# The order of A sums, raw K's turn and the merge's turns on VectorE, in a recurrence followed by a mixture of experts

## The chip, the cores and the metric

The kernel runs on one core of a Trainium2 chip. The metric is the device time of one execution in microseconds. Before the change it is 1082.37 us, the median of 3 runs (1082.31 to 1082.71).

## The reference

The first block is a recurrence over 768 tokens, for 4 batches of 8 heads with head dimension 40. Each head carries a 40 x 40 state:

```python
for t in range(S):
    kt, vt, rt = (k[:, :, t], v[:, :, t], r[:, :, t])
    wt, at, bt = (w[:, :, t], a[:, :, t], b[:, :, t])
    y[:, :, t] = np.einsum('bhd,bhde->bhe', rt, state)
    Sa = np.einsum('bhde,bhe->bhd', state, at)
    state_decay = state * wt[:, :, None, :] - np.einsum('bhd,bhe->bhde', Sa, bt)
    state = state_decay + np.einsum('bhd,bhe->bhde', vt, kt)
```

Its output, 3072 tokens of 320 numbers, goes through a mixture of 4 experts with 1024 hidden columns. The weights p are the given probabilities, divided by their sum for each token:

```python
for e in range(E):
    h = np.maximum(x @ w1[e], 0.0)
    out += p[:, e:e + 1] * (h @ w2[e])
```

Everything is float32.

## The kernel before, in words

**Units and chunks.** The recurrence is cut into chunks of 64 tokens. A unit is one chunk of two of the four batches, so there are 24 units, numbered 0 to 23, and two units make a chunk. All 8 heads of a unit are worked on at once. Units 8 and later (`BY_CHANNEL`) turn their raw inputs K and B on VectorE; earlier ones go another way.

**What a unit does.** Four generators make the instructions of a unit, a stage at a time:
- `within`: the work that needs no state. G is the running product of the decays w (a turn of raw W, a scan), gp its reciprocal (L582). RT, VT and AT are turned from raw data by `turn_raw` (L324). NT is turned from raw B and multiplied by gp (L640), KT from raw K and multiplied by gp (L645). TensorE forms the scores pc (from RT and VT), pfe (NT, AT), pe (KT, AT) and pev.
- `substitute`: solves a unit triangular system in blocks of 32. VectorE forms M (L730 to L746); GpSimd then runs 16 rounds of one product (L760) and two additions (L777) on Z, some 22 us.
- `merge`: VectorE turns Z to Qc (L793) and Qc to QTc (L794); GpSimd copies QTc into QT (L800); TensorE computes pY from QTc, then pQ from Qc.
- `step`: the work with the state. TensorE computes prn, psat, pxr and pdy; VectorE forms RH (L844), Y (L913, L919) and the new state (L924, L925). Y goes by 8 transfers on SyncE's queue into xT, the input of the mixture.

**The mixture.** It runs by chunks, one chunk behind, in pieces put between the stages above. Hidden columns come in two halves: TensorE forms ph, ScalarE writes hs with the rectifier (L978). The down product uses seven products of half blocks in place of eight. `down_1` forms p431, three products in one PSUM tile; its third term reads the sum a1. `down_2` forms p75 and p26, which read the sums a7, a5, a2 and a6. VectorE forms these five A sums from hs (`add_h`, L1104, 128x512 each, one buffer for each of the five, so a sum of one expert can be written only when the product of the expert before has read it). It also adds each product, times the gate, into osb: four operations behind p431 (L993; for a chunk's first expert two of them are L991), four behind p75 and p26 (L993). PSUM tiles of the mixture share three slots.

**Order.** Each engine runs its instructions in the order in which they stand in its queue. A scheduler lays that order out from the program order and its priorities. On VectorE it is bound further by stated edges: `tc.add_manual_dep(..., BEHIND)` puts one instruction behind another on the engine without a wait. The list `ahead_of_merge` has such edges for the units from 8 on. In it, names such as `sum_a{n}`, `Kr{u}.0` (the first turn of raw K), `K{u}` and `N{u}` (the products with gp), `Qc{u}`, `QTc{u}` and `out{n}` (the additions into osb) stand for single instructions. Before the change it has, among others, these:

```python
    ahead_of_merge = [(f"{x}{u}", f"Qc{u - 1}") for u in range(BY_CHANNEL, NU) for x in "KN"]
    ahead_of_merge += [
        (f"{x}{u}", f"sum_a{10 * (u - 1) - 50 + n}") for u in range(BY_CHANNEL, NU) for x in "KN" for n in range(5)
    ]
```

So the products N and K of unit u go ahead of five sums, and ahead of the merge of unit u - 1. These five are the second set of sums in a loop body; the first set is bound by another edge, behind gp of a later unit. The main loop (`for u in range(1, NU)`) emits, for u of 5 or more: the stages of unit u's `step`, `gap(1)` (two pieces of the mixture), the first stage of the merge of unit u + 1, and so on.

Of the kernel before, what the change touches and what calls it, by code (L numbers as in the profile page):

```python
# [33 lines left out]
def kernel(  # L34
# [48 lines left out]
    NU = NC * B // 2  # L83
# [38 lines left out]
    def of_mixture(name):  # L122
# [6 lines left out]
        out=ident[:], in_=ident[:], pattern=[[1, P]], compare_op=ALU.is_equal, fill=0.0,  # L129
# [5 lines left out]
    for t, n, op in ((upf, L, ALU.is_gt), (diagf, Q, ALU.is_equal)):  # L135
        nc.vector.memset(t, 1.0)
        for q in range(P // n):
            o = slice(q * n, (q + 1) * n)
            nc.gpsimd.affine_select(
                out=t[o], in_=t[o], pattern=[[1, n]], compare_op=op, fill=0.0, base=0, channel_multiplier=-1,  # L140
# [71 lines left out]
    BY_CHANNEL = 8  # L212
# [101 lines left out]
    def go(moves, eng=None):  # L314
        for move in moves:
            move(eng or nc.sync)
# [471 lines left out]
    def merge(q):  # L788


        Qc = sb.tile([P, H, Q], FP32, name="Qc", tag="q", bufs=2)
        QTc = sb.tile([P, H, Q], FP32, name="QTc", tag="q", bufs=2)
        keep(noted(nc.vector.transpose(out=dealt(Qc[:]), in_=q.Z), "Qc", q.u))  # L793
        ins = nc.vector.transpose(  # L794
            out=QTc[:].rearrange("p h r -> p (h r)"), in_=Qc[:].rearrange("p h c -> p (h c)"),
        )
        keep(noted(ins, "QTc", q.u))
        q.QT = QTs()
        for i in range(P // Q):
            ins = nc.gpsimd.tensor_copy(out=q.QT[quarter(i), :, quarter(i % 2)], in_=QTc[quarter(i)])  # L800
            tc.keep_in_program_order(ins)
        yield

        def two_heads(name, lhsT, rhs, to):
            p = (of_mixture if q.u == 0 and name == "pY" else big)(name)
            for n in range(NJ):
                for r in range(2):
                    matmul(
                        out=p[half(r), n * 2 * Q:(n + 1) * 2 * Q], lhsT=lhsT[half(r), 2 * n:2 * n + 2, :],
                        rhs=rhs[half(r), 2 * n:2 * n + 2, :], start=True, stop=True,  # L810
                    )
            for r in range(2):
                for y in range(2):
                    src = p[quarter(2 * r + y), 0:H * Q].rearrange("p (n two t) -> p n two t", two=2, t=Q)[:, :, y, :]
                    with sooner(name == "pY"):
                        ins = nc.scalar.copy(out=of_slot(to[quarter(2 * r)], y), in_=src)
                    noted(ins, name + "c", q.u, 2 * r + y)

        Y = Ys()
        two_heads("pY", q.below, QTc, Y)  # L820
        yield

        two_heads("pQ", Qc, Y, q.QT[:, :, quarter(1)])
        yield
# [348 lines left out]
    def begin_later(n):  # L1173
        for move in later[:n]:
            tc.keep_in_program_order(move(nc.sync))
        del later[:n]

    def mix(n):

        for piece in todo[:n]:  # L1180
            ready = stores[:]
            del stores[:]
            piece()
            for begin_store in ready:
                begin_store()
            begin_later(6 if here[0] % 4 == 0 and n > 1 else 3 if n > 1 else 6)
        del todo[:n]
# [5 lines left out]
    def run(gen, n=99):  # L1193
        if gen is None:
            return
        for _ in range(n):
            if next(gen, gen) is gen:
                break
# [3 lines left out]
    def begin_step(u):  # L1202
        q = units[u]
        if q.bp == 0:
            chunks_x[q.c] = sb.tile([P, 3, 2 * P], FP32, name="xT", tag="xT", bufs=2)
        q.xT = chunks_x[q.c][:, :, q.bp * P:(q.bp + 1) * P]
        return step(q, q.xT)
# [40 lines left out]
    m, s = merge(units[0]), begin_step(0)  # L1248
# [37 lines left out]
    m, s = merge(units[1]), begin_step(1)  # L1286
# [24 lines left out]
    for u in range(1, NU):  # L1311
        in_order[0] = True
        q = units[u]
        m = s_next = w = w_next = iter(())
        if u + 1 < NU:
            m, s_next = merge(units[u + 1]), begin_step(u + 1)
            w_next = ws[u + 1]
        if u + 2 < NU:
            w = ws[u + 2]

        def gap(n, pieces=None):
            here[0] = at = 4 * u + n
            run(sum_ops, sums_at.get(at, 0))
            mix((1 if at in sparse else 2) if pieces is None else pieces)

        early = u < EARLY
        if early:
            begin_later(len(later))
        ahead = u + 3 < NU and u >= EARLY
        if ahead and u < EARLY + 3:  # L1330
            go(load_raw(begin(u + 3), "W"))
        if early:
            lead()
        if u == 1:
            run(s, 1)
            run(w_next)
        else:
            run(w_next, 99 if early else 1)
            if u == EARLY:
                lead()  # L1340
            run(s, 1)
        gap(0)


        if early:
            run(s, 1)
        run(w, 1)
        if not early:
            run(w_next)
            run(s, 1)  # L1350
            if BY_CHANNEL <= u + 2 < NU:
                load_tokens(units[u + 2])
            run(s)

        if early:
            run(w, 1)
            gap(1, 2 if u + 1 == EARLY else None)
            run(s)
        if u == 1:
            mixture_of_unit(q)  # L1360
        elif q.bp:
            mixture_of_chunk(units[u - 1:u + 1], chunks_x[q.c])
        if not early:
            begin_later(len(later))
            run(w, 1)
            lead()
            todo[:2] = todo[1::-1]
            gap(1)
            run(m, 1)

        if u + 3 < NU:
            if u == 1:
                go_now(load_raw(begin(4), "WVRA"))
            else:
                go(load_raw(units[u + 3] if ahead else begin(u + 3), "A" if ahead else "WA"))
            load(units[u + 3], "V" if u + 3 >= BY_CHANNEL else "WBKV")
            if u > 1:
                later.extend(load_raw(units[u + 3], "VR"))
        run(w, 2)
        if BY_CHANNEL <= u + 2 < NU:  # L1380
            scale_tokens(units[u + 2])

        soon = u in (2, 3, 4)
        if soon:
            run(w, 1)
        if early:
            run(m, 1)
        else:
            run(m, 1)
            run(s_next, 1)  # L1390
            lead()
            run(m, 1)
            if u + 3 < NU:
                ws.append(within(units[u + 3]))
                run(ws[u + 3], 1)
        if soon:
            substitute(units[u + 2], nc.gpsimd)
        gap(2)

        if u == 1:  # L1400
            run(s_next, 1)
            run(m, 1)
        if not soon:
            run(w, 1)
        if not soon and u + 2 < NU:
            with sooner(not early):
                substitute(units[u + 2], nc.gpsimd)
        if not early:
            lead()
            run(s_next, 1)  # L1410
        if early:
            run(w, 1)
        if early:
            ws.append(within(units[u + 3]))
            run(ws[u + 3], 1)
            if u > 1:
                run(m, 1)
                run(s_next, 1)
            run(m)
            if u == 3:  # L1420
                begin_later(len(later))
            gap(3, 1)
            run(s_next, 1)
        else:
            if BY_CHANNEL <= u + 3 < NU:
                if u + 3 == BY_CHANNEL:
                    pad_raw()
                later.extend(load_raw(units[u + 3], "BK"))
            begin_later(len(later))
            gap(3)  # L1430
        if u >= EARLY + 2 and u + 4 < NU:
            later.extend(load_raw(begin(u + 4), "W"))
        s = s_next
    mix(len(todo))
    for piece in last:
# [4 lines left out]
    waits_of_scalar = [(f"SXc0.{n}", "RTc1.0") for n in range(4)]  # L1440
    ahead_of_merge = [(f"{x}{u}", f"Qc{u - 1}") for u in range(BY_CHANNEL, NU) for x in "KN"]
    ahead_of_merge += [
        (f"{x}{u}", f"sum_a{10 * (u - 1) - 50 + n}") for u in range(BY_CHANNEL, NU) for x in "KN" for n in range(5)
    ]
    ahead_of_merge += [(f"VC{u}.{r}", f"1/gp{u + 1}") for u in range(BY_CHANNEL, NU - 1) for r in range(2)]
    ahead_of_merge += [(f"RH{u - 1}.{r}", f"1/gp{u + 1}") for u in range(BY_CHANNEL, NU - 1) for r in range(2)]
# [1 line left out]
    ahead_of_merge += [(f"QTc{u - 1}", f"VC{u}.{r}") for u in range(BY_CHANNEL, NU) for r in range(2)]  # L1448
    ahead_of_merge += [(f"1/gp{u + 2}", f"sum_a{10 * u - 45 + n}") for u in range(BY_CHANNEL, NU - 2) for n in range(5)]
    ahead_of_merge += [(f"Z2{u}", f"AT{u + 1}") for u in range(BY_CHANNEL, NU - 1)]  # L1450
    in_second = [("Zr1.14", "out0"), ("out0", "Zm1.16")]
    for one, then in [*zip(names, names[1:]), *((f"out{n}", x) for n, x in moved), ("blocks0.3", "VCv1"), ("blocks0.3", "ETc0.0"), ("blocks1.3", "Zu1.0"), ("blocks1.3", "Zu1.3"), *turned_ahead, *in_second, *waits_of_scalar, *ahead_of_merge]:
        tc.add_manual_dep(made[then].ins, made[one].ins.name, BEHIND, reason="stated order of VectorE")
# [30 lines left out]
```

## Time and profile before

The profiled execution took 1082.07 us; the span from its first to its last instruction is 1080.3 us. The mean granted TensorE clock is 0.998.

| engine | busy us | share of the span | instructions |
|---|---|---|---|
| PE (TensorE), matmuls | 1053.6 | 98% | 16022 |
| PEld (TensorE), weight loads | 944.2 | 87% | 16022 |
| DVE (VectorE) | 801.6 | 74% | 1565 |
| ACT (ScalarE) | 344.2 | 32% | 942 |
| POOL (GpSimd) | 527.6 | 49% | 1322 |

Weight loads overlap matmuls. Matmuls are pipelined, so consecutive ones overlap in the timelines, and a busy PE is not PE at its peak. Rows of a timeline give start, length (both us), engine, line and operation, out<-in with partitions x elements, and in brackets the idle time of the engine just before with what ended it. Rows of the waits give the engine and line that waited, what it waited for, then us in total, times and the longest in us. Rows of the chain of work that ended last give start, length and what ran.

In the steady part a pair of units takes 85.2 us. The table follows the operations that the change names, in the loop body whose merge is that of unit 11 (odd) and in the next one (unit 12, even); starts in us.

| operation on VectorE | merge 11 | merge 12 |
|---|---|---|
| second product's last addition (L993) | 433.71 | 475.81 |
| turns of raw K (L324) | 434.01 | 479.43 |
| K times gp (L645) | 434.81 | 480.46 |
| five A sums (L1104) | 435.41 to 439.08 | 481.07 to 484.26 |
| Y (L913) | 439.00 | 477.32 |
| first down product's four additions | 441.60 to 443.19 | 484.19 to 485.77 |
| Qc (L793) | 443.11 | 485.69 |
| QTc (L794) | 443.76 | 486.33 |

### The profile page before, as it was taken

The page shows a single profiled execution, that of the slowest core. Times are in us where ns is not written, and L with a number is a line of the kernel's source. Part 1 is how long each engine was busy: PE and PEld are TensorE (multiplying, and loading weights), DVE is VectorE, ACT ScalarE, POOL GpSimd, SP SyncE. Part 2 cuts the span into 40 slices and gives each one's busy share as a digit, 9 for nine tenths or more (in the row PEclk, how much of TensorE's full clock was granted, in tenths as well). Part 3 has the DMA queues.
Part 4 walks back from the last instruction along what each step waited for, and adds up shares of the span by engine and source line. Part 5 has one row for each costly group of instructions (what it writes and reads, how often), then busy time and mean ns, then how long its engine had stood idle before and what let it go on. Part 6 is the DMA issues. An engine that isn't in the chain of part 4 may idle for free.

```text
span 1080.3 us, 38526 instructions
## 1 busy us (share of the span) xinstructions
PE 1053.6 (98%) x16022; PEld 944.2 (87%) x16022; DVE 801.6 (74%) x1565; ACT 344.2 (32%) x942; POOL 527.6 (49%) x1322
## 2 busy tenths in 40 slices
PE   8999999999999999999999999999999999999998
PEld 7888878888889989889989898998988998998887
DVE  7787679898777967978778779778787786634343
ACT  3433344423333323324233333232233333221110
POOL 6117777756465374464563653744735636420000
PEclk9999999999999999999999999999999999999999
DMA  6776644444444443543453353354444443121220
GB/s 119 192 202 140 138 106 112 83 101 106 109 96 109 102 113 74 131 108 78 114 126 82 88 143 71 92 133 88 99 113 101 102 104 86 53 73 51 75 85 13
DMA packets 275350, 111.05 MB, mean 103 GB/s; under 512 B 229816, under 2 KB 254952, under 8 KB 275176
## 3 DMA queue, kind: packets, MB, share of 16 engines
q1 hardware_dynamic: 271192, 107.75, 42.8%
q8 instruction: 126, 2.06, 0.8%
q10 hardware_dynamic: 3984, 0.84, 0.4%
q14 instruction: 48, 0.39, 0.1%
HBM read 100.65 MB, written 3.93 MB: 97 GB/s over the span
## 4 chain that ended last, share of the span: by engine, by line
PE 76%; DVE 10%; POOL 8%; issue 2%; DMA 2%; ACT 1%; SPq 1%; DVEq 0%; POOLq 0%
PE ph L110 33%; PE p L110 25%; POOL Z L777 5%; POOL Z L760 3%; PE pdy L110 2%; DVE a L1104 2%; PE prn L110 2%; PE po L110 2%; PE pxr L110 2%; PE psat L110 2%; PE pfe L110 1%; PE warm L110 1%; PE pc L110 1%; PE pY L110 1%; PE pe L110 1%
## 5 line engine op out<-in xcount | busy, mean ns | idle before, releaser
L777 POOL TENSOR_TENSOR Z<-Z 128x31 f32<-128x31 f32 (+7 forms) x704 | 261.1, 371 | 55.1
L110 PE MATMUL ph<-xT,w1b 128*128 128x256 f32 (+3 forms) x1536 | 222.4, 374 | 0.5 <-issue 0.5
L978 ACT ACTIVATE hs<-ph 128x512 f32<-128x512 f32 (+1 forms) x208 | 117.0, 564 | 331.8 <-PE ph L110 329.8
L110 PE MATMUL ph<-xT,w1a 128*128 128x256 f32 (+3 forms) x1536 | 220.8, 373 | 0.0
L993 DVE SCALAR_TENSOR_TENSOR osb<-p,gate,osb 128x320 f32<-128x320 f32 (+1 forms) x243 | 108.2, 482 | 133.1 <-PE p L110 130.9
L760 POOL TENSOR_TENSOR Z<-M,Z 128x62 f32<-128x62 f32 (+7 forms) x352 | 149.6, 425 | 95.3 <-DVE M L746 69.6
L110 PEld LDWEIGHTS ph<-xT,w1b 128*128 128x128 f32 (+1 forms) x1536 | 168.8, 161 | 27.8 <-issue 7.0
L110 PEld LDWEIGHTS ph<-xT,w1a 128*128 128x128 f32 (+1 forms) x1536 | 167.9, 161 | 28.3 <-issue 6.7
L1104 DVE TENSOR_TENSOR a<-hs 128x512 f32<-128x512 f32 x220 | 148.8, 710 | 41.2 <-ACT hs L978 41.2
L110 PE MATMUL p<-sums,a 128*128 128x160 f32 x1056 | 165.7, 300 | 9.7 <-DVE a L1104 9.7
L110 PEld LDWEIGHTS p<-sums,a 128*128 128x128 f32 x1056 | 152.6, 190 | 13.6 <-DVE a L1104 11.4
L727 POOL COPY below<-F 32x256 f32<-32x256 f32 x48 | 20.6, 430 | 177.4 <-ACT F L670 175.8
L110 PEld LDWEIGHTS p<-w,hs 128*128 128x128 f32 x704 | 98.6, 190 | 9.0 <-issue 7.8
L110 PE MATMUL p<-w,hs 128*128 128x160 f32 x704 | 104.9, 302 | 0.5 <-DVE osb L993 0.5
L110 PE MATMUL p<-w,a 128*128 128x160 f32 x704 | 102.8, 299 | 0.0
L110 PEld LDWEIGHTS p<-w,a 128*128 128x128 f32 x704 | 98.0, 190 | 0.0
L800 POOL COPY QT<-QTc 32x256 f32<-32x256 f32 x96 | 40.3, 420 | 92.6 <-DVE QTc L794 74.9
L898 ACT COPY RS<-pxr 64x256 f32<-64x256 f32 x88 | 32.3, 367 | 104.7 <-DVE SX L499 92.6
L582 DVE RECIPROCAL gp<-G 128x512 f32<-128x512 f32 x16 | 53.6, 3353 | 0.5
L730 DVE STREAM_TRANSPOSE M<-blocks 128x1024 f32<-128x1024 f32 x24 | 47.4, 1975 | 3.3 <-ACT blocks L722 3.0
L708 ACT COPY EV<-pev 64x160 f32<-64x160 f32 x96 | 23.1, 286 | 83.7 <-PE pev L110 83.4
L670 ACT COPY F<-pfe 128x256 f32<-128x256 f32 x48 | 15.5, 376 | 80.1 <-PE pfe L110 77.9
(167 smaller groups left out, 1422.0 us busy)
## 6 DMA issues: line engine op xcount, KB each, us to landing
w1a<-in_moe_w_dram SPq DMA_DIRECT2D x37, 512.0 KB
w1b<-in_moe_w_dram SPq DMA_DIRECT2D x37, 512.0 KB
w<-in_moe_w_dram SPq DMA_DIRECT2D x4, 1280.0 KB
w1a<-in_moe_w_dram SPq DMA_DIRECT2D x74, 64.0 KB
w1b<-in_moe_w_dram SPq DMA_DIRECT2D x74, 64.0 KB
out_dram<-osb SPq DMA_DIRECT2D x45, 80.0 KB
rawW<-in_w_dram SPq DMA_DIRECT2D x48, 72.0 KB
natV<-in_v_dram SPq DMA_DIRECT2D x42, 80.0 KB
```

Of the source, the lines that this page charges most:

```text
L110: return stated(nc.tensor.matmul(**k))
L582: pin(noted(nc.vector.reciprocal(out=gp[:], in_=G[:, :, 1:L + 1]), "1/gp", q.u))
L708: nc.scalar.copy(out=of_slot(q.EV[half(p)], i ^ p)[:, :, 0:D], in_=pev[i][half(p)])
L727: tc.keep_in_program_order(nc.gpsimd.tensor_copy(out=q.below[quarter(i)], in_=q.F[quarter(i), :, 0:Q]))
L730: ins = nc.vector.transpose(out=M[:], in_=cols)
L760: ins = eng.tensor_tensor(out=Z[:, 1:3, 0:n, j + 1:Q], in0=M[:, j:j + 2, None, j + 1:Q].to_broadcast([P, 2, n, m]), in1=Z[:, here, 0:n, j: ...
L777: eng.tensor_tensor(out=z[:, 0], in0=z[:, 0], in1=z[:, x], op=ALU.add)
L800: ins = nc.gpsimd.tensor_copy(out=q.QT[quarter(i), :, quarter(i % 2)], in_=QTc[quarter(i)])
L898: nc.scalar.copy(out=RS[half(s), x ^ s::2], in_=prs[x][half(s)].rearrange("p (j i) t -> p j i t", i=2),)
L978: ins = nc.scalar.activation(out=h[:, i * HF // 2:(i + 1) * HF // 2, 0:n], in_=ph[i][:], func=ACTF.Relu,)
L993: ins = nc.vector.scalar_tensor_tensor(out=to, in0=p, scalar=sc, in1=to, op0=ALU.mult, op1=ALU.add)
L1104: ins = nc.vector.tensor_tensor(out=t[:], in0=x, in1=y, op=op)
```

## The change

The five sums go ahead of the first turn of raw K and are no longer bound behind N. For odd units from 9 on, the first stage of the merge is emitted ahead of `gap(1)`; new edges put QTc ahead of the four additions of a chunk's first down product, and Y and the new state of unit u - 1 ahead of Qc.

```diff
@@ main loop @@
             todo[:2] = todo[1::-1]
+            merge_first = u + 1 > BY_CHANNEL and u % 2 == 0
+            if merge_first:
+                run(m, 1)
             gap(1)
-            run(m, 1)
+            if not merge_first:
+                run(m, 1)
@@ stated order of VectorE @@
     ahead_of_merge += [
-        (f"{x}{u}", f"sum_a{10 * (u - 1) - 50 + n}") for u in range(BY_CHANNEL, NU) for x in "KN" for n in range(5)
+        (f"sum_a{10 * (u - 1) - 50 + n}", f"Kr{u}.0") for u in range(BY_CHANNEL, NU) for n in range(5)
     ]
...
     ahead_of_merge += [(f"Z2{u}", f"AT{u + 1}") for u in range(BY_CHANNEL, NU - 1)]
+    ahead_of_merge += [(f"QTc{u}", f"out{16 * u - 72 + n}") for u in range(BY_CHANNEL + 1, NU - 1, 2) for n in range(4)]
+    ahead_of_merge += [(f"{x}{u - 1}.{n}", f"Qc{u}") for u in range(BY_CHANNEL + 1, NU - 1, 2) for x in ("Y", "SG") for n in range(2)]
```

## The prediction

> **What bounds the kernel now.** I read the page first, then the waits of TensorE, then the timelines of TensorE, VectorE and GpSimd over one pair of units (430 to 520 us), then the chain there.
>
> ```profile
> span 1080.3 us, 38526 instructions
> PE 1053.6 (98%) x16022; PEld 944.2 (87%) x16022; DVE 801.6 (74%) x1565; ACT 344.2 (32%) x942; POOL 527.6 (49%) x1322
> PE 76%; DVE 10%; POOL 8%; issue 2%; DMA 2%; ACT 1%; SPq 1%; DVEq 0%; POOLq 0%
> ```
>
> TensorE (PE) sets the end. It is without work for 1080.3 - 1053.6 = 26.7 us, so no reordering of VectorE can gain much more than that. The waits of TensorE say where those microseconds lie (us in total, times, longest):
>
> ```profile
> PE p L110 <- DVE a L1104: 9.7, 7, 1.4
> PE pY L110 <- DVE QTc L794: 2.4, 4, 1.5
> ```
>
> I name a stretch of the trace by the unit whose merge (Qc, QTc, pY) falls in it; the loop body then stands one unit behind. Seven equal waits for a product's A sum lie in the even stretches 10 to 22 (at 396.68, 481.85, 567.09, 652.62, 737.84, 823.01 and 908.21 us, 85 us apart), and small ones for the turn QTc. TensorE's timeline in stretch 12 (first kind), and in stretch 11 (second kind; start, length, idle before in brackets):
>
> ```profile
> 478.07 2.44 PE L110 MATMUL p<-w,hs 128*128 128x160 f32 x16
> 481.85 1.35 PE L110 MATMUL p<-sums,a 128*128 128x160 f32 x8 [1.34 <-DVE a L1104]
> ...
> 444.35 0.59 PE L110 MATMUL pY<-QTc,below 64*64 64x64 f32 x13 [0.23 <-issue]
> ```
>
> VectorE in the same two places (stretch 12 first):
>
> ```profile
> 480.46 0.69 DVE L645 TENSOR_TENSOR KT<-KT,gp 128x512 f32<-128x512 f32 x1
> 481.07 3.19 DVE L1104 TENSOR_TENSOR a<-hs 128x512 f32<-128x512 f32 x5
> ...
> 441.60 1.01 DVE L991 TENSOR_SCALAR osb<-p,gate 128x320 f32<-128x320 f32 x2
> 442.52 0.67 DVE L993 SCALAR_TENSOR_TENSOR osb<-p,gate,osb 128x160 f32<-128x160 f32 x2
> 443.11 0.62 DVE L793 STREAM_TRANSPOSE Qc<-Z 128x256 f32<-128x256 f32 x1
> 443.76 0.45 DVE L794 STREAM_TRANSPOSE QTc<-Qc 128x256 f32<-128x256 f32 x1
> ```
>
> At 480.5 TensorE has done two terms of p431 and wants sum a1; VectorE is still multiplying K and starts the sums at 481.07. At 444.1 pc is done (443.43 + 0.69) and pY wants QTc, which ends at 443.76 + 0.45 = 444.21 because the four L991/L993 additions ran ahead of it. The profile puts this gap down to "issue", to pc or to QTc by turns. I take QTc: in even stretches, where QTc ends 0.76 us ahead of pY (486.33 + 0.45 = 486.78 against 487.54), pY follows pc with no gap.
>
> **What each stall costs.** The chain of waits shows it as a stretch that should be equal everywhere, from the start of pdy to the start of the next dense ph:
>
> ```profile
> 433.69 1.51 PE pdy L110 x59
> 439.61 3.45 PE ph L110 x16
> ...
> 475.67 1.51 PE pdy L110 x59
> 483.20 3.45 PE ph L110 x16
> 490.44 3.65 PE ph L110 x16
> ```
>
> Without the stall it is 439.61 - 433.69 = 5.92; with it 483.20 - 475.67 = 7.53. The seven stretches give 7.53, 7.53, 7.63, 7.58, 7.61, 7.55, 7.59, sum 53.02; less 7 x 5.92 = 41.44 that is **11.6 us** (the idle time alone is 9.7; the rest is the pipeline draining and filling). For pY the stretch is from that ph to the next: 490.44 - 483.20 = 7.24 in even stretches, 447.29 - 439.61 = 7.68 in odd ones (TensorE's next 3.65 us of ph there starts at 447.29). Seven odd merges (units 9 to 21, pY at 359.18, 444.35, 529.50, 615.03, 700.26, 785.48, 870.65) lose 0.45 each, the one at 615.03, idle for 0.53 and not 0.23, 0.75: 6 x 0.45 + 0.75 = **3.4 us**.
>
> **The change part by part.** It adds and removes no instruction. By the order of instructions on each engine only VectorE's changes: TensorE, ScalarE, GpSimd and SyncE keep theirs, so no DMA is issued in another place and GpSimd's four QT copies keep their turn.
>
> *Sums ahead of raw K, sixteen times (K of units 8 to 23).* Before, N and K (turns 2 x 0.4, products 0.7) stood ahead of the five sums. Now the sums stand between RT and the second product's additions, N partly behind them, K behind all. Can they run there? a1 needs the last hs: ScalarE ends it at 470.76 + 0.60 = 471.36, when VectorE is idle (to 472.93). a7, a5, a2 and a6 overwrite sums that p75 and p26 still read; these products run from 470.56 to 475.0. The first five sums of a unit already run like this, between additions (452.23 to 456.48, behind products that end at 455.2). So the last sum ends near 476.5, a1 near 472.1: 8 us before TensorE wants it at 480.5. The stall goes whole: 11.6 us. What is late next? The additions of p75 and p26 slip by up to 1 us; the dense pool's three PSUM slots they free are taken at 476.94 and 478.07, so this is covered. Y starts at 477.32 behind pdy; up to 0.5 us late, its xT transfers begin 13 us before their use. K ends near 482; KT is read by pe at 507.73. Raw K is free 1 to 3 us later, and its next load is issued at 500.16 (even) or 465.22 (odd), about 20 us later; nothing on SP's queue waits. In odd stretches (sums at 435.41 before) nothing on TensorE waited; Y moves from 439.00 to about 436, its xT sends with it. No gain, no cost. The sums of K8 and K9 (259 and 308 us) show no stall either.
>
> *Qc and QTc ahead of the four additions, odd merges 9 to 23.* Qc cannot start before Z: GpSimd's last Z operation ends at 441.06 + 0.52 = 441.58. So Qc goes from 443.11 to 441.65, 1.46 us earlier and not the 1.68 of the additions; QTc ends at 442.75, 1.4 us before pY wants it. The 3.4 us go. VectorE now waits at Qc from about 439.5 with the additions behind it; they end at 444.4, or near 446.2 where VC's two copies, which wait for pc, come between. Their PSUM slot is wanted by p75 at 450.78: covered. RH, at 446.07 before, then comes 0.1 to 0.5 us late against TensorE, and with it G, gp, M and the next Z. That eats into the next even stretch's margin: below. Unit 23's Qc already waits for Z (0.39 us) and no gap of TensorE stands there: nothing.
>
> *The margin of GpSimd's Z in even stretches.* VectorE's operations with two operands in SBUF slow Z. In stretch 11 the five sums at 435.41 lengthen these rows (in stretch 12 the same forms take 0.66 and 0.62):
>
> ```profile
> 435.81 1.32 POOL L777 TENSOR_TENSOR Z<-Z 128x49 f32<-128x49 f32 x2
> 437.94 1.27 POOL L777 TENSOR_TENSOR Z<-Z 128x35 f32<-128x35 f32 x2
> ```
>
> With the L760 rows between, five sums cost Z some 1.8 us, 0.36 each. In stretch 12 Z ends at 483.12, about three sums already in it; now all five, and Z grows by two or three times 0.36, some 0.8 us, bounds 0 (they hit gaps) and 2.2 (each of five sums stops Z for its whole 0.7 us, 3.5, less the 1.3 lost already). I take 0.8, the nearest rows. Z then ends near 484.0, QTc near 485.1; with 1.4 us less stall pY wants it at 486.15, and at 485.7 once stretch 11 has lost its 0.45. Margin 0.6 us. By the Trainium skill (SBUF — State Buffer, "Who interferes with whom") a VectorE instruction with two SBUF inputs and a GpSimd instruction that reads SBUF lock each other out for a whole instruction. The doubled rows agree with a lock; that the five sums cost 1.8 and not 3.5 us does not show a full block each time. By that rule at its worst the sum would be that of rival B.
>
> **The sum.** 11.6 + 3.4 = 15.0 us off the profiled execution (1082.07 us, its span 1080.3): 1067.1. The median shown is 1082.37, 0.3 more: 1067.4. I add 0.3 for a small rest of waits in even stretches: **1067.7**.
>
> **The rivals.**
> A. Only the sums' stall goes. For: four of seven pY gaps are put down to "issue" or pc; if a wake-up costs 0.23 us whenever pY waits for two engines, it stays. Against: even stretches show none. 1082.4 - 11.6 = 1070.8.
> B. Z takes the stall over in even stretches. For: the two-operand sums land on Z wholly. With the 2.2 us bound Z ends near 485.4, QTc 486.5, pY is 0.8 to 1.0 us late, seven times: 1067.4 + 6.5 = about 1074. Against: 0.36 a sum in the rows. Between this and the forecast lies 1070.
> C. Slower than before: GpSimd sets the pace. VectorE, in order, now stops at Qc until Z is done, and RH, G, gp (3.35 us) and M, which starts the next Z, are queued behind. By the estimates above this loop has some 2 us to spare in a pair of stretches: 0.6 at QTc and 1.5 at RH (VectorE free at about 485.9, prn's result at 487.4). The pair would take 85.17 - 1.66 - 0.45 = 83.1 us on TensorE, 81 in the loop; before, it took 85.17. So it decides once the loop grows by over 4.2 us a pair. That needs every two-operand instruction beside Z (five sums, AT, N, K, Y times G: nine a stretch) to stop it for its whole 0.7 us where the rows show 0.36: 18 x 0.34 = 6.1, a pair of 87.1, 7 x 1.9 = 13 us slower, 1096. Against: stretch 11 carries all nine already, and its Z takes 22.3 us (419.24 to 441.58).
> That the change does nothing is out: the order on VectorE does move.
>
> **Chances.** Forecast 0.72 (own range 1066 to 1069.5), A 0.11, B and what lies between 0.13, C 0.04, most of it slower. The range, 1066.0 to 1072.5, leaves out C, the worst half of B and a gain beyond the 15 us. About 0.2% (2.2 us) can be told from no change. Faster comes from forecast, A and B, 0.96; within 0.2%, 0.01, and slower, 0.03, from C, mild or whole.
>
> **What would show it.** TensorE's waits without "p <- a" at seven places; from pdy to ph 5.92 us everywhere, ph to ph 7.24 in odd stretches too; Qc of odd merges starting just behind the last Z; Z of even merges under 23 us. Wrong would be: pY waiting for QTc in even stretches (B), or Qc waiting for Z longer and longer (C).

## The result, and the profile after

The changed kernel takes **1067.48 us** (median of 4 runs, 1067.07 to 1067.69), the kernel before beside it 1082.34 (1081.73 to 1082.71): a ratio of 0.9863, 95% interval 0.9846 to 0.988. The prediction was 1067.7, with a range of 1066.0 to 1072.5. The profiled execution takes 1067.27 us where 1067.1 was worked out for it. The same changed kernel took 1066.06 us in a second set of runs (below), so a difference of a microsecond or so between sets of runs tells little.

Three lines of the page of the changed kernel (span; busy time of the engines; shares of the chain that ended last):

```profile
span 1065.6 us, 38523 instructions
PE 1050.4 (99%) x16022; PEld 942.9 (88%) x16022; DVE 800.6 (75%) x1565; ACT 344.1 (32%) x942; POOL 537.7 (50%) x1322
PE 83%; POOL 8%; DVE 5%; issue 2%; ACT 1%; DMA 1%; SPq 1%; DVEq 0%; POOLq 0%
```

TensorE's and VectorE's busy times are nearly those of before. What went is TensorE's idle time, from 26.7 us to 1065.6 - 1050.4 = 15.2, and VectorE's share of the chain, from 10% to 5%. So 11.5 of the 14.7 us are idle time; the other 3.2 are busy time, which the prediction had counted by taking the whole stretch from pdy to ph and not the idle time alone. GpSimd is busy 10.1 us longer; 9.8 of it in Z's operations, the price that the sums put on Z.

The waits of TensorE (total, times, longest) have lost their first row, "p <- DVE a". What they start with now is from the first 280 us, before the steady part:

```profile
PE pc L110 <- ACT RT L553: 2.0, 2, 1.6
PE warm L110 <- POOL ident L128: 1.8, 1, 1.8
PE pY L110 <- DVE QTc L794: 1.3, 2, 1.2
```

Stretches of 160 us of the changed kernel (busy time and instructions of PE, PEld, DVE, ACT, POOL; then granted clock, DMA share, GB/s). PE was busy for 158.19, 156.42 and 156.76 us in these before, and is now busy throughout:

```profile
400.00:560.00 160.00, 160.00 (x2606) 145.84 (x2605) 129.68 (x243) 54.59 (x151) 89.83 (x217) 1.00 0.48 107
560.00:720.00 160.00, 160.00 (x2508) 145.89 (x2507) 129.03 (x244) 54.02 (x147) 88.41 (x218) 1.00 0.46 103
720.00:880.00 160.00, 160.00 (x2608) 145.84 (x2606) 131.60 (x251) 52.77 (x146) 88.53 (x217) 1.00 0.46 105
```

The chain of the changed kernel in stretches 11 and 12:

```profile
431.89 1.51 PE pdy L110 x59
...
437.81 3.45 PE ph L110 x16
...
445.04 3.65 PE ph L110 x16
...
473.42 1.51 PE pdy L110 x59
...
479.34 3.45 PE ph L110 x16
...
486.57 3.65 PE ph L110 x16
```

From pdy to ph it is 437.81 - 431.89 = 5.92 in the odd stretch and 479.34 - 473.42 = 5.92 in the even one (7.53 before); from that ph to the next 7.23 in both (7.68 in odd ones before). All merges from 9 to 21 read so, within 0.01. A pair of stretches takes 83.1 us instead of 85.2.

VectorE in the same places, the odd merge first:

```profile
440.40 0.63 DVE L793 STREAM_TRANSPOSE Qc<-Z 128x256 f32<-128x256 f32 x1 [2.80 <-POOL Z L777]
...
441.06 0.45 DVE L794 STREAM_TRANSPOSE QTc<-Qc 128x256 f32<-128x256 f32 x1
...
469.13 1.55 DVE L1104 TENSOR_TENSOR a<-hs 128x512 f32<-128x512 f32 x2 [2.61 <-ACT hs L978]
...
481.77 0.63 DVE L793 STREAM_TRANSPOSE Qc<-Z 128x256 f32<-128x256 f32 x1 [0.20 <-POOL Z L777]
482.43 0.45 DVE L794 STREAM_TRANSPOSE QTc<-Qc 128x256 f32<-128x256 f32 x1
```

The sums of stretch 12 start at 469.13 and not at 481.07. Qc waits for Z in both kinds of merge, 2.80 us and 0.20 us. QTc ends at 441.51 and 482.88; TensorE starts pY at 442.14 and 483.68. So QTc is 0.6 and 0.8 us ahead (over merges 9 to 22, from 0.6 to 1.2): Z with the two turns behind it is the next thing that can stop TensorE. Where pY waited for QTc in the kernel before, it started 0.15 us behind QTc's end, so not all of that margin can be used up.

### The profile page after: what moved, and what is told of

Its sections match the earlier page's. It is cut to its first block, busy times and chain, and to the rows that moved or that the text cites. A ratio compares the mean times of both kernels' runs of the same rounds, so it can differ in the third digit from the quotient of the medians.

```text
span 1065.6 us, 38523 instructions
## 1 busy us (share of the span) xinstructions
PE 1050.4 (99%) x16022; PEld 942.9 (88%) x16022; DVE 800.6 (75%) x1565; ACT 344.1 (32%) x942; POOL 537.7 (50%) x1322
## 4 chain that ended last, share of the span: by engine, by line
PE 83%; POOL 8%; DVE 5%; issue 2%; ACT 1%; DMA 1%; SPq 1%; DVEq 0%; POOLq 0%
PE ph L110 36%; PE p L110 29%; POOL Z L777 5%; POOL Z L760 3%; PE pdy L110 3%; PE psat L110 2%; PE prn L110 2%; PE po L110 2%; PE pxr L110 2%; PE pfe L110 1%; PE pc L110 1%; PE warm L110 1%; PE pev L110 1%; PE pe L110 1%; PE pQ L110 1%
## 5 line engine op out<-in xcount | busy, mean ns | idle before, releaser
L1104 DVE TENSOR_TENSOR a<-hs 128x512 f32<-128x512 f32 x220 | 154.6, 721 | 78.6 <-ACT hs L978 78.6
L760 POOL TENSOR_TENSOR Z<-M,Z 128x62 f32<-128x62 f32 (+7 forms) x352 | 160.5, 456 | 94.6 <-DVE M L746 68.8
L993 DVE SCALAR_TENSOR_TENSOR osb<-p,gate,osb 128x320 f32<-128x320 f32 (+1 forms) x243 | 107.7, 480 | 69.8 <-PE p L110 66.5
L793 DVE STREAM_TRANSPOSE Qc<-Z 128x256 f32<-128x256 f32 x24 | 15.0, 626 | 40.8 <-POOL Z L777 40.6
```

What stands on the lines that cost most here:

```text
L760: ins = eng.tensor_tensor(out=Z[:, 1:3, 0:n, j + 1:Q], in0=M[:, j:j + 2, None, j + 1:Q].to_broadcast([P, 2, n, m]), in1=Z[:, here, 0:n, j: ...
L993: ins = nc.vector.scalar_tensor_tensor(out=to, in0=p, scalar=sc, in1=to, op0=ALU.mult, op1=ALU.add)
L1104: ins = nc.vector.tensor_tensor(out=t[:], in0=x, in1=y, op=op)
```

## The experiments

The kernel before ran beside each of these: 1082.2 us for edit 1 alone, edit 2 alone, only a1 and unit 7's merge with both edits; 1082.69 for the late turns and the sums with one operand; 1082.51 for the last two.

**Edit 1 alone** (sums ahead of raw K, the merge where it was).

```diff
-            merge_first = u + 1 > BY_CHANNEL and u % 2 == 0
+            merge_first = False
...
-    ahead_of_merge += [(f"QTc{u}", f"out{16 * u - 72 + n}") for u in range(BY_CHANNEL + 1, NU - 1, 2) for n in range(4)]
-    ahead_of_merge += [(f"{x}{u - 1}.{n}", f"Qc{u}") for u in range(BY_CHANNEL + 1, NU - 1, 2) for x in ("Y", "SG") for n in range(2)]
```

> Only the sums' new place is kept; the merge's first stage stands behind the four additions again, as before the change. Theory 'two stalls, two edits' (the prediction's): the seven waits for a1 are gone (11.6 us), the seven gaps before pY in odd stretches stay at 0.2 us idle and 0.45 us of stretch each (3.4 us): about 1070.8 us. Rival 'one edit does both': in the changed kernel VectorE stands idle from 437.60 to 440.40 waiting for Z, and p431 is done at about 437.9, so the four additions (1.6 us) fit ahead of the end of Z anyway; Qc starts at Z's end in either order: about 1067.5 us, no gap before pY. I expect the rival.

Measured: 1066.5 us (1065.78 to 1067.65), ratio 0.985 (0.9833 to 0.9868). The whole gain is there without the merge edit. VectorE in stretch 11 of this run:

```profile
438.15 1.01 DVE L991 TENSOR_SCALAR osb<-p,gate 128x320 f32<-128x320 f32 x2
439.07 0.67 DVE L993 SCALAR_TENSOR_TENSOR osb<-p,gate,osb 128x160 f32<-128x160 f32 x2
440.70 0.62 DVE L793 STREAM_TRANSPOSE Qc<-Z 128x256 f32<-128x256 f32 x1 [0.96 <-POOL Z L777]
```

The additions still stand ahead of Qc, but they end at 439.7 and Qc waits for Z until 440.70. In the kernel before, the sums ran from 435.41 to 439.08 with Y behind them, so that the additions began only at 441.60, just as Z ended (441.58). With the sums gone from there, Y and the additions move up some 3 us, and fit in the wait for Z.

**Edit 2 alone** (the merge's turns ahead, the sums behind N and K as before).

```diff
-        (f"sum_a{10 * (u - 1) - 50 + n}", f"Kr{u}.0") for u in range(BY_CHANNEL, NU) for n in range(5)
+        (f"{x}{u}", f"sum_a{10 * (u - 1) - 50 + n}") for u in range(BY_CHANNEL, NU) for x in "KN" for n in range(5)
```

> Only the merge's new place is kept; N and K stand ahead of the sums again. Theory: QTc in odd stretches ends at about 442.75, the gaps before pY go, 3.4 us off the kernel before: about 1079.0 us, with the seven waits for a1 left at 1.3 to 1.4 us each. Rival 'given back': VectorE's loop sets the start of a1, so that what pY gains is lost at the next a1: about 1082.3 us, a1 waits of 1.8 us each. A third outcome, over 1083, would say that additions behind Qc make something late.

Measured: 1082.06 us (1079.88 to 1087.79 in 12 runs), ratio 1.0001 (0.9987 to 1.0015); the profiled execution takes 1085.13. The odd gaps are gone: ph to ph is 447.71 - 440.48 = 7.23 in stretch 11. But nothing is left of the 3.4 us. The first of TensorE's waits in this run, and the wait in stretch 12:

```profile
PE p L110 <- DVE a L1104: 11.4, 7, 2.1
```

```profile
483.04 1.35 PE L110 MATMUL p<-sums,a 128*128 128x160 f32 x8 [2.11 <-DVE a L1104]
484.23 5.30 PE L110 MATMUL ph<-xT,w1b 128*128 128x256 f32 x16
```

Two things took it. In stretches 12, 16 and 20 of this run N's turns stand behind the additions of p26 (at 476.66 in stretch 12), Y starts later (478.07 and not 477.32), and a1 keeps TensorE 2.11, 1.97 and 1.94 us: 1.7 us more in all. And the ph behind the 2.11 us takes 5.30 where it takes 3.6 elsewhere. Stretches of this run around the waits of 2.11 us and 1.94 us (columns as above):

```profile
480.95:484.36 3.41, 1.32 (x9) 1.32 (x10) 3.38 (x7) 0.00 (x0) 1.26 (x4) 1.00 0.33 63
484.36:487.77 3.41, 3.41 (x10) 2.66 (x9) 3.38 (x8) 0.03 (x1) 0.00 (x0) 0.50 0.19 51
822.28:825.70 3.42, 2.35 (x16) 2.10 (x16) 3.20 (x9) 0.00 (x0) 2.79 (x9) 1.00 0.45 78
825.70:829.11 3.41, 2.54 (x15) 2.39 (x16) 3.41 (x7) 0.00 (x0) 0.81 (x2) 1.00 0.25 51
829.11:832.52 3.41, 3.41 (x57) 2.94 (x57) 2.32 (x7) 1.51 (x3) 0.82 (x3) 1.00 0.24 57
```

The granted clock is 0.50 for the 3.41 us behind a stretch of 3.41 in which PE was idle for 2.09, and stays at 1.00 where the same wait falls into two such stretches (idle 1.07 and 0.87). Three such stretches at 0.50 stand in this execution between 270 and 1000 us, none in those of before and after; each costs half of 3.41, 1.7 us. Two of them stand behind a1 waits; the third stands behind unit 7's merge, where PE was idle for 1.48 us in one stretch, against 1.47 in the kernel before, which had no half clock there: that one is chance. The account: - 3.4 + 1.7 + 3 x 1.7 = + 3.4 against 1085.13 - 1082.07 = + 3.1. Executions with a mean clock of 0.999 took 1079.9 and 1080.0, near the 1079.0 that was expected, and the one at 0.991 took 1087.79.

**Only a1 ahead** (the four other sums behind N and K as before, no merge edit).

```diff
-        (f"sum_a{10 * (u - 1) - 50 + n}", f"Kr{u}.0") for u in range(BY_CHANNEL, NU) for n in range(5)
+        (f"sum_a{10 * (u - 1) - 50}", f"Kr{u}.0") for u in range(BY_CHANNEL, NU)
+    ]
+    ahead_of_merge += [
+        (f"{x}{u}", f"sum_a{10 * (u - 1) - 50 + n}") for u in range(BY_CHANNEL, NU) for x in "KN" for n in range(1, 5)
```

> Of the five sums only a1 goes ahead of raw K; the other four stay behind K; the merge as before the change. Theory 'a1 alone': TensorE waited for a1 alone, so the seven waits go and the time is about 1067.5 us. Theory 'all five': a1's wait goes, but K and the four sums (0.7 + 2.5 us) still stand ahead of the four additions and Qc in even stretches, so QTc ends about 0.6 us after pY wants it: seven gaps before pY of 0.4 to 0.8 us and about 1071 to 1073 us. I expect 'all five'.

Measured: 1069.27 us (1069.14 to 1069.89), ratio 0.9876 (0.9859 to 0.9893). The a1 waits are gone, and small ones ahead of pY stand in even stretches. VectorE and TensorE in stretch 12 of this run:

```profile
478.60 2.68 DVE L1104 TENSOR_TENSOR a<-hs 128x512 f32<-128x512 f32 x4
...
482.71 0.61 DVE L793 STREAM_TRANSPOSE Qc<-Z 128x256 f32<-128x256 f32 x1
```

```profile
483.94 0.59 PE L110 MATMUL pY<-QTc,below 64*64 64x64 f32 x13 [0.20 <-PE pc L110]
```

Four sums and the four additions ahead of Qc bring QTc to 483.80, just too late; the same kind of gap that odd merges had before. In even stretches ph to ph is 7.66 us and not 7.23 as in odd ones (7.74 in stretch 14), some 3.1 us in seven. So a1 alone removes the seven long waits, and moving the other four sums is worth the last 2.8 us (1069.27 against 1066.5 for edit 1 alone, run beside it), less than the 3.5 to 5.5 us that were expected.

**The merge's turns made late** by one, three and six more turns of Z (0.6 us each) ahead of Qc, for merges 9 to 23. The edit with three:

```diff
-        keep(noted(nc.vector.transpose(out=dealt(Qc[:]), in_=q.Z), "Qc", q.u))
+        [keep(noted(nc.vector.transpose(out=dealt(Qc[:]), in_=q.Z), "Qw", q.u, n)) for n in range(3 if q.u > BY_CHANNEL else 0)]; keep(noted(nc.vector.transpose(out=dealt(Qc[:]), in_=q.Z), "Qc", q.u))
...
+    ahead_of_merge += [(x, f"Qw{y[2:]}.{n}") for x, y in list(ahead_of_merge) if y[:2] == "Qc" and int(y[2:]) > BY_CHANNEL for n in range(3)]
```

> The changed kernel with one more turn of Z (0.62 us on VectorE) ahead of Qc in the merges of units 9 to 23, so that QTc comes 0.62 us later in each. Theory (TensorE sets the pace; in the trace of the changed kernel QTc ends 0.8 us before pY wants it in odd merges and 1.0 us before in even ones): the delay fits in both margins, no gap of TensorE, 1067 to 1068.5 us. Rival (the loop through GpSimd's Z, Qc, RH, gp and M has no slack left after the change): every merge hands its 0.62 us on, 15 x 0.62 = 9 us, about 1076 to 1077.

Measured: 1068.39 us (1067.84 to 1069.05), TensorE busy 480.00 of 480 us between 400 and 880. One turn fits, just: in stretch 11 pY starts 0.15 us behind QTc's end, without a gap of TensorE. The loop through Z hands nothing on.

> The same with three more turns, 3 x 0.62 = 1.9 us. Theory: QTc comes about 1.1 us too late in odd merges and 0.9 in even ones; with the 0.2 us that a gap costs beside its idle time in the trace of the kernel before, 8 x 1.3 + 7 x 1.1 = 18 us, about 1085 (1081 to 1089), and the waits of TensorE show pY behind QTc some 15 times at about 1 us. Rival (no slack in the loop through Z): 15 x 1.9 = 28 us, about 1095. If the margins are far wider than read off (over 2 us): no change.

Measured: 1086.59 us (1084.88 to 1086.61). TensorE waits ahead of pY in all 15 merges, 0.73 to 1.19 us and once 1.78, 14.8 us together. The wait in stretch 11 of this run:

```profile
444.80 0.59 PE L110 MATMUL pY<-QTc,below 64*64 64x64 f32 x13 [1.10 <-DVE QTc L794]
```

So the margin is what the trace shows, between one and three turns; two turns more than fit undo the whole gain of the change.

> The same with six more turns, 3.7 us: gaps of about 2.8 us ahead of pY, 15 times. It asks whether a gap of TensorE of this length brings half clock, as in the run with the merge edit alone, where gaps of 1.5 to 2.1 us were followed by 3.41 us at half clock in three of four places. If it does nearly every time: 15 x (2.9 + 1.7) = 69 us, about 1136, with a granted clock below 0.9 in the slices behind the gaps and ph rows longer than 3.65. If gaps of this length don't bring it: 15 x 2.9 = 44 us, about 1111, ph rows as before.

Measured: 1134.74 and 1140.03 us; mean clock 0.976 and 0.971. Stretches of the first, around three of the 15 waits:

```profile
449.61:453.02 3.41, 1.13 (x64) 1.16 (x67) 3.31 (x8) 0.40 (x2) 1.03 (x3) 1.00 0.24 65
453.02:456.43 3.41, 3.41 (x63) 2.97 (x55) 3.36 (x8) 1.29 (x6) 2.23 (x4) 0.50 0.94 253
...
773.91:777.32 3.41, 1.64 (x87) 1.67 (x90) 2.22 (x5) 0.87 (x4) 1.50 (x4) 1.00 0.48 95
777.32:780.74 3.42, 3.42 (x42) 3.02 (x35) 3.27 (x6) 1.91 (x8) 1.76 (x3) 1.00 0.38 68
```

Behind a stretch with 2.28 us idle the clock is 0.50, behind one with 1.77 it is 1.00. The 15 waits add up to 44.0 us, and 14 stretches of 3.41 us at 0.50 stand behind ten of them: 44.0 + 14 x 1.7 = 67.8, against 1134.74 - 1067.27 = 67.5.

**Sums with one operand.** Each A sum is replaced by a turn of its first operand; the second operand is left out.

```diff
-                ins = nc.vector.tensor_tensor(out=t[:], in0=x, in1=y, op=op)
+                ins = nc.vector.transpose(out=t[:], in_=x)
```

> The changed kernel with each A sum replaced by a turn of its first operand alone (128x512, one operand, about 0.7 us on VectorE, as long as the sum); the second operand of every sum is left out. If VectorE's second SBUF operand is what slows GpSimd's Z, as the prediction took it (0.36 us a sum, five sums a stretch): Z falls from 22.7 to about 21 us in even and odd stretches alike, its L777 rows of 1.3 us go back to about 0.65, and QTc's margin grows by 1.8 us. If the busy VectorE slows it whatever the operand count: Z stays at 22.7. The time stays near 1067.5 us by both, since TensorE sets it.

Measured: 1063.64 us, one run. Z falls from 22.9 to 20.6 us in stretch 11 and from 22.7 to 20.2 in stretch 12. Over merges 9 to 22 it falls by 1.5 to 2.5 us, 2.0 in the mean: 0.30 to 0.50 us for each of five sums, 0.39 in the mean. The turns take 0.69 us on VectorE, nearly as long as the sums (0.72). GpSimd's last Z operation of stretch 11 in this run, and VectorE's turns behind it:

```profile
433.79 0.52 POOL L777 TENSOR_TENSOR Z<-Z 128x8 f32<-128x8 f32 x2
```

```profile
434.35 0.62 DVE L793 STREAM_TRANSPOSE Qc<-Z 128x256 f32<-128x256 f32 x1 [1.08 <-POOL Z L777]
...
435.00 0.45 DVE L794 STREAM_TRANSPOSE QTc<-Qc 128x256 f32<-128x256 f32 x1
```

QTc ends at 435.45 and pY starts at 438.36: a margin of 2.9 and not 0.6. So it is the sum's kind, not VectorE's busy time, that slows GpSimd. The trace of the changed kernel says which trait. In merges 9 to 22, 279 Z operations ran beside VectorE instructions with at most one operand in SBUF alone (turns, the additions L993, and Y at L913, which adds one operand in PSUM to one in SBUF). Each took at most 0.012 us more than the shortest of its kind, 0.002 in the mean, as did those with no VectorE instruction beside them. The 212 beside an instruction with two operands in SBUF (the sums, N and K times gp, Y and the state times G) took 0.21 us more in the mean and up to 0.55. L913 is of the same kind of operation as the sums, so it is the second operand in SBUF that counts. The time fell by 3.6 us, which neither theory expected. From stretch 11 on the two kernels keep step (pdy to pdy 41.53 in both); the lead was won earlier: 1.4 us by 38 us, where this execution has no half clock and the changed kernel's has 6.8 us of it; 1.0 by 264 us, in short waits; and 1.4 at unit 7's merge, where QTc then comes in time. The first of these is chance, as the section on the prediction shows.

**Unit 7's merge**, the one wait left. `Z2{u}` is VectorE's last operation on M, which GpSimd's Z reads. That of unit 7 is put ahead of unit 8's turns of A and V on VectorE, so that GpSimd can start Z earlier; both edits stay in. (The expectation of the later run with edit 1 and this step calls the operations moved GpSimd's last Z operations; it is VectorE's Z2 that moves.)

```diff
-    ahead_of_merge += [(f"Z2{u}", f"AT{u + 1}") for u in range(BY_CHANNEL, NU - 1)]
+    ahead_of_merge += [(f"Z2{u}", f"{x}T{u + 1}") for u in range(BY_CHANNEL - 1, NU - 1) for x in "AV" if x == "A" or u < BY_CHANNEL]
```

> The changed kernel, and for unit 7 M and Z2 go ahead of unit 8's turns of A and V, as in later units. In the changed kernel pY of unit 7 waits 1.19 us for QTc behind a late Z; M of unit 7 stands behind 0.69 + 0.69 + 0.65 us of unit 8's work. Theory: Z of unit 7 ends about 1.9 us earlier, the gap goes, about 1066.1 us, 0.1% below the changed kernel and at the edge of what can be measured; the trace shows it. Rival: AT or VT of unit 8 becomes late, 1067.5 us or more.

Measured: 1065.85 us (1064.46 to 1066.26), ratio 0.9839 (0.9821 to 0.9856). PE is busy 159.50 of 160 us between 240 and 400, where it was 158.31.

The same step with edit 1 only, and the changed kernel beside it on one chip:

> The sums ahead of raw K (edit 1) and, at unit 7's merge, GpSimd's last Z operations ahead of two turns of unit 8 (as in the run with both edits and this step), but without the merge edit. If the merge edit is worth nothing once the sums are ahead, as the run with edit 1 alone showed: the same time as the version with it, 1065 to 1066.5, about 1.2 us under the changed kernel run beside it, and no gap of TensorE between 280 and 950 us. If the merge edit is worth its 3.4 us in this order: 1068 to 1070.

> The changed kernel itself, beside the one above on the same chip, since the times of the runs with edit 1 alone (1066.5) and of the changed kernel (1067.5) are from two chips. 1066.5 to 1067.7 if they are one and the same; if the merge edit costs a microsecond of its own, it stays at 1067.5 and the version without it at 1065.

Measured: 1065.34 us (1064.88 to 1066.12) without the merge edit, ratio 0.9837 (0.9815 to 0.9859), and 1066.06 (1065.38 to 1066.85) for the changed kernel. The merge edit is worth nothing that can be told once the sums are ahead, and costs nothing that can be told. Among the kernels that compute the whole result this is the lowest time of the study, by less than the intervals.

## Why the prediction was right, point by point

- **Seven a1 stalls, 11.6 us: right.** They are gone, pdy to ph is 5.92 everywhere, and the run with edit 2 alone, which leaves them, gains nothing.
- **Seven odd pY gaps, 3.4 us: right in size, wrong in cause.** The prediction's step "Qc and QTc ahead of the four additions ... The 3.4 us go" gave them to the merge edit. Edit 1 alone removes them. The step that failed is "In odd stretches (sums at 435.41 before) nothing on TensorE waited ... No gain, no cost": it followed Y and its transfers to their new place, but not the additions behind Y, which then end ahead of Z. The sum came out all the same because both edits were in the kernel; for edit 1 alone the same working gives 1070.8, and 1066.5 was measured. Either edit alone closes the gap, so the terms don't add up from single edits: 15.7 us for edit 1, 0 for edit 2 (where half clock and longer a1 waits took what the gap gave), 14.9 for both. Rival A, 1070.8 for the sums' stall alone, is out for the same reason.
- **Z in even stretches: right.** It grew by 0.8 by the forecast, by 22.7 - 21.8 = 0.9 in stretch 12 (0.7 to 1.5 in the even ones from 10 to 22, and it stays under 23 us). QTc's margin was forecast at 0.6 us and is 0.8 to 1.1. In odd stretches a margin of 1.4 was forecast, and 0.6 came in stretches 11, 15 and 19, where Z grew too, from 22.3 to 22.9; in 9, 13, 17 and 21, with a Z of 22.4 to 22.5, it is 1.1 to 1.2. Rival B needed Z to lose 2.2 us; its mechanism is real (the runs with late turns show what it costs), but the size is not reached.
- **The loop through GpSimd, rival C: not reached.** A turn more in 15 merges cost 0.9 us between the medians, not 9, and TensorE never waited for it between 400 and 880 us. One step of the rival's own working is off: with 83.1 us a pair on TensorE and 81 in the loop, the loop sets the pace once it grows by 2.1 us a pair; 4.2 is where the kernel gets slower than before.
- **The 0.3 us kept back for small waits: not there.** In its place the profiled execution of the changed kernel lost 1.0 us at the start (first pdy at 38.78, before at 37.74), with 6.8 us of half clock there and 3.4 before. This is chance and not the change: in the twelve traces the first pdy starts at 37.4 to 37.6 with no half clock there, at 37.7 with 3.4 us of it and at 38.6 to 38.9 with 6.8, the changed kernel among the last both times; runs that hold the whole change stand in all three groups. By unit 8 the loss had shrunk to 0.3 us. From there on the kernel won 15.1 us, where 15.0 was worked out. That the totals agree within 0.2 us is luck too, since the same kernel took 1066.06 us in its second set of runs.

## What to carry to other kernels

When TensorE waits at two places for one in-order engine, look at what each moved instruction frees behind its old place as well as what it delays at its new one: one move may close both gaps, and the terms of two edits then don't add up. Try each edit alone before both are kept. Where a chain on other engines has under a microsecond to spare, measure it by putting known work into it: one turn cost nothing here, three undid the change.

## What the runs showed of the hardware

The granted clock of TensorE goes by fixed stretches of 3.41 us: in every trace the changes of clock lie a whole number of them apart. In the two runs with long waits, behind 300 us, each such stretch with 1.95 us or more of PE's idle time was followed by one at 0.50 (twelve cases), and none with 1.88 or less, unless its own clock was already 0.50. At unit 7's merge, among other matmuls, 1.48 us was enough once and 1.47 was not. The Trainium skill (TensorE: Matmul & The Clock Gate, "Part 1: The HAM clock gate") has the free-running window of 3413 ns, which these traces show too, and it puts half clock behind an idle window. The rule of thumb of the Trainium skill (TensorE: Matmul & The Clock Gate, "Why this matters for your kernels") is to leave no gaps over some 3 us. Here a window idle for little over half was enough, and a wait of 2.0 us cost some 3.7 (2.0 and 1.7 of half clock) when it fell into one window and 2.0 when it was split. Waits near that length therefore spread the times of a kernel: the 12 executions of edit 2 alone took 1079.88 to 1087.79 us, from a mean clock of 0.999 for the shortest to 0.991 for the longest, while the eight of the changed kernel, in two sets, took 1065.38 to 1067.69. Not every spread comes from the clock: the kernel before took 1081.1 to 1086.11 us in 17 executions beside edit 2, with a mean clock of 0.998 in both of these; that cause stays open.

The sums' price for GpSimd is 0.30 to 0.50 us of the 0.7 that each takes, 0.39 in the mean, by the run with one operand; the forecast had 0.36, from rows of one stretch, and was near it. The lock of the Trainium skill (SBUF — State Buffer, "Who interferes with whom") agrees in direction: a VectorE instruction with one SBUF operand left Z alone (148 Z operations beside the turns took at most 0.01 us more than the shortest of their kind), and one with two slowed it, but did not stop it for its whole length on average.
